# Second stage of a fused attention and two-layer expert kernel: loads of h moved to the queue of weights and stores, weights in four transfers, next pool opened with the last products' issue

## The chip, the cores and the metric

The kernel runs on one core of a Trainium2 chip. The metric is device time in microseconds (us) of one execution; lower is better. TensorE (PE) multiplies, its weight loads are PEld; ScalarE is ACT, VectorE is DVE, GpSimd is POOL, and SyncE (SP) issues transfers. ACTq and SPq are the transfers that ScalarE and SyncE issue.

## The reference

```python
x = attention(q, k, v)                       # 4 x 8 heads, 576 tokens of 64: pooled plus local part
x = x.transpose(0, 2, 1, 3).reshape(2304, 512)
h = (x @ w_a) * (x @ w_b)                    # 2304 x 1536
x2 = h @ w_out                               # 2304 x 512: the second stage here
h2 = x2 @ moe2_w_in                          # 2304 x 2048
out = (h2 * clip(h2 + 3, 0, 6) / 6) @ moe2_w_out
```

All in 32-bit floats. The inputs of the weights come as 64-bit words, which the kernel decodes.

## The kernel before

Each matrix product is made of three matmuls of split operands (`PASSES`): a tile holds a rounded first part (a copy by ScalarE) and the rest (a subtraction by VectorE). So each operand passes ScalarE, then VectorE, then TensorE.

The first stage makes attention and h, and stores h in DRAM, as 12 arrays `h_d[f]` of 128 rows and 2304 columns. The second stage (`second`, line 636) takes the tokens in five spans, four of 512 and one of 256. For each span it goes through f = 0 to 11: load 128 rows of h (`load`, line 641), the first part on ScalarE (line 647), the rest on VectorE (line 651), then 12 matmuls on TensorE into four banks of sums (`products`, line 659). A load of h is 256 KB, in the last span 128 KB. h has four buffers: three (`hg0`) that f = 0, 1, 2, 4, 5, 6, 8, 9, 10 take in turn, and one (`hg1`) for f = 3, 7, 11. Since that one is free later, the products run in the order 0, 1, 2, 4, 3, 5, 6, 8, 7, and so on. At a span's end ScalarE copies the four sums to `x2f` (line 676) and SyncE stores them (line 683).

Beside this the weights of the third and fourth stage are decoded: `decode` (line 223) loads 1 MB into a tile `raw` (two buffers, line 229), ScalarE makes `m` (line 237), and VectorE does six operations (lines 243 to 261). `pieces` (w2i) makes sums of quarters and splits them into `w2`; `staged` (w2o, line 1034) makes seven combinations in `ws` and stores them in DRAM (`w_d`, line 1065).

The third stage (`inner`, line 711) loads x2 in pairs of blocks (`x2r`, line 719), splits it into `in` (lines 699 and 702), and multiplies (`ph`, line 772); the fourth (`outer`) makes the output. Their tiles lie in the pool `p4`, which takes the place of the earlier pools of h, wo and raw. Before, it is opened behind the end of the last product, the issue of all stores of x2 and of all stores of w_d.

What sets the order: `Plan` holds every step with an engine, a planned duration, a due time (`want`), what it waits for, and buffers that it takes and gives. It runs the steps in planned time, on each engine the ready one with the smallest due time, and the instructions are issued in that order. Each engine, and each queue of transfers, keeps it. All transfers are planned on one queue, at 256 KB per us and 2.5 us more until they land, whichever engine issues them:

```python
def DMA(kb, want, run, after=(), take=(), give=()):
    i = plan.add("SP", dma(kb), want, run, after, take)
    j = plan.add("-", 0, want, lambda: None, [i], give=give, late=DMA_L)
    issued[j] = i
```

Before, the loads of h are planned so but issued by ScalarE, the others by SyncE. In the compiled program all transfers share eight completion counters, taken in turn: a transfer is not issued before the eighth ahead of it has landed.

Of the kernel before, what the change touches and what calls it, by code (L numbers as in the profile page):

```python
# [138 lines left out]
def fused_kernel(ctx: ExitStack, tc: tile.TileContext, qk, vt, vd, wab, wo, w2i, w2o, mask, out):  # L139
# [44 lines left out]
    def slot(pool, shape, dtype, tag, name):  # L184
        return pool.tile(shape, dtype, tag=tag, bufs=BUFS[tag], name=name)
# [8 lines left out]
    def act(n):  # L194
        return 0.1 + 0.00095 * n
# [26 lines left out]

    def decode(src, want, put, tag, after=(), ahead=4, slack=1.0, raw=None, queue=None):

        T = {}

        def load():
            T["raw"] = slot(xp if raw == "x" else dp, [P, W], mybir.dt.uint64, raw or "raw", "raw")
            (queue or nc.sync).dma_start(T["raw"].rearrange("p (a c) -> p a c", a=CUT), src.rearrange("a p c -> p a c"))

        def words():
            w = T["raw"].bitcast(U32).rearrange("p (n t) -> p n t", t=2)
            return w[:, :, 0], w[:, :, 1]
# [35 lines left out]


        i = DMA(1024, want - ahead, load, take=[raw or "raw"])
        i = ACT(act(W), want, magnitude, [i], take=["dm"], slack=slack)
        i = DVE(2 * dve2(W), want, exponent, [i])
# [9 lines left out]

    def pieces(src, want, where, raw=None):


        i, words = decode(src, want, None, None, slack=1.0, raw=raw)
        Q = W // CUT

# [347 lines left out]
    def second(n, f, want):  # L637
# [3 lines left out]
        def load():  # L641
            h = hs[n, f] = hg_slot(f, "h")[:, :, :nb]
            nc.scalar.dma_start(h[:, 1].bitcast(F32), h_d[f][:, lo:hi])

# [8 lines left out]
        def products():  # L653
            if f == 0:
                accs[n] = [bank("acc")[:, :nb] for _ in range(KC)]
            for e in range(KC):
# [4 lines left out]

        stored = [S_["h", m, f] for m in range(NBLK) if begin[m] < hi and begin[m] + sizes[m] > lo]
        i = DMA(nb // 2, want - 12, load, stored + [S_["p3" if f % 4 == 3 else "p2"]], take=[f"hg{f % 4 // 3}"])
        i = ACT(act(nb), want - 12, h_first, [i])
        i = DVE(dve(nb), want - 12, h_second, [i])
        i = S_["second", n, f] = PE(12 * (0.009 + 0.00044 * nb), want, products, [i, S_["wo", f // 2], S_["ps"]],
               take=["q"] * KC if f == 0 else [],
               give=[f"hg{f % 4 // 3}"] + (["wo"] if n == len(spans) - 1 and f % 2 else []))
        if f < F1 - 1:
            return  # L670
        for e in range(KC):
            T = {}

            def out_of(e=e, T=T):
                T["t"] = slot(pools["p3"], [P, NC], F32, "xo", "x2f")[:, :nb]
                nc.scalar.activation(T["t"], accs[n][e], AF.Copy)

            def store(e=e, T=T):
                for m in range(lo // NB, (hi - 1) // NB + 1):
                    if m not in x2_d:  # L680
                        x2_d[m] = dram.tile([KC, P, NB], F32, name=f"x2_d{m}")
                    a, b = max(lo, m * NB), min(hi, m * NB + NB)
                    nc.sync.dma_start(x2_d[m][e][:, a - m * NB:b - m * NB], T["t"][:, a - lo:b - lo])

            j = ACT(act(nb), want, out_of, [i], take=["xo"], give=["q"])
            j = DMA(nb // 2, want, store, [j], give=["xo"])
            for m in range(lo // NB, (hi - 1) // NB + 1):
                S_.setdefault(("x2d", m), []).append(j)
        S_["last second"] = i

# [19 lines left out]
    def inner(p, want, opened):  # L710
# [3 lines left out]

        def load(t, h):
            def run():
# [3 lines left out]
            return DMA(NB, want - 12 if p else want - 6, run,  # L720
                       S_["x2d", m[t]] + [S_["second", len(spans) - 1, 1] if p == 0 else opened],
                       take=["x0" if p == 0 else "L"])


        ld = {(h, t): load(t, h) for t, h in ((0, 0), (1, 0), (1, 1), (0, 1))}
        tag = "x0" if p == 0 else "L"
# [241 lines left out]
    for f in range(F1):  # L968
        S_["wab", f] = decode(wab[f], when[0, f] - 4, lambda f=f: wab_t.setdefault(f, slot(wpool, [P, 2, W], F32R, "wh", "wh")),
                              "wh", ahead=26 if f < 2 else 6, slack=0.0,  # L970
                                queue=None)
    for t, (n, f) in enumerate(jobs):
# [53 lines left out]
    for i in range(F2 // 2):  # L1026
        if i == 5:
            S_["p3"] = plan.add("-", 0, 0, open_p3, [S_["h", n, f] for n, f in jobs[-2:]] + [S_["raw x", k] for k in SPARE])
        S_["raw x", i] = pieces(w2i[i], T1 + 8 + 5.5 * i, place_of(i), "x" if i in SPARE else None)
        S_["w2i", i] = S_["raw x", i]  # L1030
# [4 lines left out]
    def staged(k, want):  # L1035
        i, words = decode(w2o[k], want, None, None, slack=1.0)
        T = {}
# [45 lines left out]
    for k, (n, f) in enumerate(steps):  # L1083
        second(n, f, T2 + k)
    T3 = T2 + len(steps)
    S_["p4"] = plan.add("-", 0, 0, open_p4, [S_["last second"]] +
                        [issued[x] for m in range(2 * PAIRS) for x in S_["x2d", m]] +
                        [issued[x] for k in range(F2 // 2) for x in S_["w_d", k]])
    for p in range(PAIRS):
# [91 lines left out]
```

## Time and profile before

| | us |
|---|---|
| three runs: median (lowest, highest) | 962.59 (960.75, 963.54) |
| the profiled execution | 964.17 |
| its span, first to last instruction | 962.2 |
| TensorE busy in the span | 932.5 (97%) |
| TensorE weight loads | 875.6 (91%) |
| VectorE | 755.3 (78%) |
| ScalarE | 455.8 (47%) |

The span is the time from the first to the last instruction that the profiler recorded; the 2.0 us between it and the execution's time lie around it. Busy times overlap: the engines work at the same time. TensorE's busy time holds the modelled ends of pipelined matmuls, so a stretch in which it is busy may still hold fewer matmuls than another of the same length.

### The profile page before, as it was taken

The numbers are of one execution on the slowest core, as the hardware profiler recorded it, in microseconds if no ns is written. First come the engines' busy times: TensorE is split into PE (matmuls) and PEld (weight loads), VectorE is DVE, ScalarE is ACT, GpSimd is POOL, SyncE is SP. The second block draws the span as 40 slices with busy tenths as digits, with TensorE's granted clock in tenths as the row PEclk, the third lists the DMA queues.
The fourth block names the chain that finished last, engine by engine and source line by source line (L and its number), as shares of the span: only waits on it lengthen the run. The fifth ranks groups of instructions, "written<-read, shape, count | busy, mean of one in ns | idle before, by whom it ended". The sixth has DMA issues, their size and how long they took to land.

```text
span 962.2 us, 18896 instructions
## 1 busy us (share of the span) xinstructions
PE 932.5 (97%) x7246; PEld 875.6 (91%) x7246; DVE 755.3 (78%) x1375; ACT 455.8 (47%) x1164; POOL 5.6 (1%) x44
## 2 busy tenths in 40 slices
PE   7899999999999999999999897999999999999998
PEld 6688989999899999997778687999999999999998
DVE  4999999824637969676787842999898999897983
ACT  4677445433645333323444432555454565554551
POOL 1000000000000000000000000000000000000000
PEclk9799999999999999999999999999999999999999
DMA  9645664424115524326768756334237891805401
GB/s 268 183 124 161 196 203 138 135 84 158 43 53 167 178 95 133 131 97 224 234 196 270 233 166 202 126 132 156 107 132 263 280 289 34 277 21 188 142 17 50
DMA packets 103146, 151.23 MB, mean 157 GB/s; under 512 B 8208, under 2 KB 71696, under 8 KB 103056
## 3 DMA queue, kind: packets, MB, share of 16 engines
q1 hardware_dynamic: 93728, 134.64, 43.4%
q10 hardware_dynamic: 9328, 15.39, 5.3%
q8 instruction: 57, 0.93, 0.4%
q14 instruction: 33, 0.27, 0.1%
HBM read 100.19 MB, written 49.81 MB: 156 GB/s over the span
## 4 chain that ended last, share of the span: by engine, by line
PE 84%; DVE 8%; DMA 6%; issue 1%; ACT 1%; ACTq 0%; SPq 0%; DVEq 0%
PE pab L602 32%; PE ph L772 18%; PE oacc L895 15%; PE acc L659 10%; DMA h<-h_d 4%; PE po L543 2%; PE dsc L398 2%; DVE in L702 2%; PE sc L496 1%; PE pt L529 1%; PE dpo L448 1%; DMA raw<-w2o 1%; DVE e L868 1%; PE po L539 1%; PE dpt L430 1%
## 5 line engine op out<-in xcount | busy, mean ns | idle before, releaser
L602 PE MATMUL pab<-x,wh 128*128 128x344 f32 (+2 forms) x2016 | 319.8, 317 | 0.1
L602 PEld LDWEIGHTS pab<-x,wh 128*128 128x128 f32 x2016 | 306.4, 188 | 3.6 <-issue 1.8
L895 PE MATMUL oacc<-w2o,in 128*128 128x256 f32 x1512 | 182.0, 283 | 1.4 <-DVE in L702 1.4
L895 PEld LDWEIGHTS oacc<-w2o,in 128*128 128x128 f32 x1512 | 181.3, 191 | 2.1 <-DVE in L702 2.0
L772 PE MATMUL ph<-in,w 128*128 128x384 f32 x1008 | 175.7, 335 | 2.2 <-ACT in L699 2.1
L772 PEld LDWEIGHTS ph<-in,w 128*128 128x128 f32 x1008 | 175.2, 188 | 2.7 <-ACT in L699 2.3
L659 PE MATMUL acc<-h,wo 128*128 128x512 f32 (+1 forms) x720 | 156.5, 378 | 10.7 <-ACT h L647 9.6
L659 PEld LDWEIGHTS acc<-h,wo 128*128 128x128 f32 x720 | 127.6, 193 | 39.7 <-ACT h L647 11.8
L788 DVE TENSOR_TENSOR part<-ph,part 128x384 f32<-128x384 f32 x168 | 86.0, 553 | 8.9 <-PE ph L772 8.2
L611 DVE TENSOR_TENSOR a<-a,pab 128x344 f32<-128x344 f32 (+2 forms) x84 | 41.4, 494 | 58.2 <-PE pab L602 43.3
L796 ACT ACTIVATE r<-part,three 128x384 f32<-128x384 f32 x96 | 56.3, 613 | 53.5 <-DVE part L788 51.1
L651 DVE TENSOR_TENSOR h<-h 128x512 fp32r<-128x512 f32 (+1 forms) x60 | 37.5, 636 | 49.1 <-ACT h L647 48.9
L608 ACT ACTIVATE a<-pab 128x344 f32<-128x344 f32 (+2 forms) x84 | 36.7, 443 | 79.4 <-PE pab L602 56.9
L699 ACT ACTIVATE in<-gr 128x384 fp32r<-128x384 f32 x96 | 47.5, 521 | 41.1 <-PE oacc L895 28.6
L647 ACT ACTIVATE h<-h 128x512 fp32r<-128x512 f32 (+1 forms) x60 | 34.8, 588 | 65.5 <-DMA h<-h_d 50.8
L237 ACT ACTIVATE m<-raw 128x1024 f32<-128x1024 f32 x34 | 39.2, 1153 | 51.1 <-DVE raw L255 26.0
L702 DVE TENSOR_TENSOR in<-gr,in 128x384 fp32r<-128x384 f32 x96 | 50.0, 560 | 7.0 <-ACT in L699 6.3
L699 ACT ACTIVATE in<-e 128x384 fp32r<-128x384 f32 x72 | 36.4, 526 | 34.0 <-PE oacc L895 19.5
L799 DVE SCALAR_TENSOR_TENSOR r<-r,part 128x384 f32<-128x384 f32 x96 | 50.6, 553 | 1.3 <-ACT r L796 1.1
L513 ACT ACTIVATE e<-sc,mx 128x64 f32<-128x64 f32 x160 | 48.0, 320 | 5.3 <-DVE mx L505 5.3
L255 DVE SCALAR_TENSOR_TENSOR raw<-raw,m 128x1024 f32<-128x1024 uint32 x34 | 41.7, 1227 | 1.2
L248 DVE SCALAR_TENSOR_TENSOR raw<-raw,m 128x1024 uint32<-128x1024 uint32 x34 | 41.5, 1221 | 0.2
(86 smaller groups left out, 900.5 us busy)
## 6 DMA issues: line engine op xcount, KB each, us to landing
g_d<-r SPq DMA_DIRECT2D x96, 192.0 KB, 2.1
gr<-g_d SPq DMA_DIRECT2D x48, 384.0 KB, 5.1
raw<-wab SPq DMA_DIRECT2D x12, 1024.0 KB, 11.9
h<-h_d ACTq DMA_DIRECT2D x48, 256.0 KB, 3.8
h_d<-a SPq DMA_DIRECT2D x48, 172.0 KB, 2.0
raw<-w2i SPq DMA_DIRECT2D x8, 1024.0 KB, 5.5
raw<-w2o SPq DMA_DIRECT2D x8, 1024.0 KB, 7.3
qk<-qk SPq DMA_DIRECT2D x14, 576.0 KB, 5.9
```

The lines of the kernel that those rows point to most:

```text
L248: nc.vector.scalar_tensor_tensor(out=hi, in0=hi, scalar=0xC0000000, in1=T["m"].bitcast(U32), op0=ALU.bitwise_and, op1=ALU.bitwise_or)
L255: nc.vector.scalar_tensor_tensor(out=lo.bitcast(F32), in0=lo, scalar=2.0 ** -52, in1=m, op0=ALU.mult, op1=ALU.mult)
L513: nc.scalar.activation(L["e"][:, p, h], L["s4"][:, p, h], AF.Exp, bias=L["mx"][:, p, h:h + 1], scale=SCALE, accum_out=L["z"][:, p, h:h + 1])
L602: nc.tensor.matmul(T[k], wab_t[f][:, x, c], xs[n][:, g, y, :nb], start=(g == 0 and i == 0), stop=(g == KC - 1 and i == 2))
L659: nc.tensor.matmul(accs[n][e], wo_t[f // 2][:, x, c], hs[n, f][:, y], start=(f == 0 and i == 0), stop=(f == F1 - 1 and i == 2))
L699: nc.scalar.activation(x[0][:, 0], src(), AF.Copy)
L702: nc.vector.tensor_tensor(x[0][:, 1], src(), x[0][:, 0], op=ALU.subtract)
L772: nc.tensor.matmul(acc[k], t[:, x, g * P:(g + 1) * P], X[k, g][0][:, y], start=(g == 0 and n == 0), stop=(g == 1 and n == 2))
L788: nc.vector.tensor_tensor(s[name], acc[k], s[other], op=ALU.add)
L796: nc.scalar.activation(T["r"], src(), AF.Relu, bias=three)
L799: nc.vector.scalar_tensor_tensor(out=T["r"], in0=T["r"], scalar=6.0, in1=src(), op0=ALU.min, op1=ALU.mult)
L895: nc.tensor.matmul(acc[n][e], X[n, k][0][:, x, e * P:(e + 1) * P], t[:, y], start=(k == 0 and i == 0), stop=(k == K - 1 and i == 2))
```

## The change

The loads of h are issued by SyncE, and their due time is 40 steps ahead of the product's instead of 12; ScalarE's and VectorE's part of h are due 14 steps ahead instead of 12. All eight weights w2o and the last four of the eight w2i are loaded in four transfers of 256 KB, which take their places in the queue one by one; `m` waits for all four. The last three products of the last span are planned as issued early, and `p4` is opened behind the issue of the last one, no longer behind its end; the last span's four `x2f` lie in `p4`. The four loads of x2r for the first pair are tied to four products (the eighth, tenth and so on from the last wide span on) instead of one.

```diff
@@ decode @@
-    def decode(src, want, put, tag, after=(), ahead=4, slack=1.0, raw=None, queue=None):
+    def decode(src, want, put, tag, after=(), ahead=4, slack=1.0, raw=None, step=CUT):
...
-        def load():
-            T["raw"] = slot(xp if raw == "x" else dp, [P, W], mybir.dt.uint64, raw or "raw", "raw")
-            (queue or nc.sync).dma_start(T["raw"].rearrange("p (a c) -> p a c", a=CUT), src.rearrange("a p c -> p a c"))
+        def load(a, b):
+            def run():
+                if a == 0:
+                    T["raw"] = slot(xp if raw == "x" else dp, [P, CUT, W // CUT], mybir.dt.uint64, raw or "raw", "raw")
+                nc.sync.dma_start(T["raw"][:, a:b], src[a:b].rearrange("a p c -> p a c"))
+            return run
...
-        i = DMA(1024, want - ahead, load, take=[raw or "raw"])
-        i = ACT(act(W), want, magnitude, [i], take=["dm"], slack=slack)
+        i, loads = None, []
+        for a in range(0, CUT, step):
+            i = DMA(256 * step, want - ahead, load(a, a + step), [i and issued[i]], take=[] if a else [raw or "raw"])
+            loads.append(i)
+        i = loads
+        i = ACT(act(W), want, magnitude, i, take=["dm"], slack=slack)
@@ second @@
-            nc.scalar.dma_start(h[:, 1].bitcast(F32), h_d[f][:, lo:hi])
+            nc.sync.dma_start(h[:, 1].bitcast(F32), h_d[f][:, lo:hi])
...
-        i = DMA(nb // 2, want - 12, load, stored + [S_["p3" if f % 4 == 3 else "p2"]], take=[f"hg{f % 4 // 3}"])
-        i = ACT(act(nb), want - 12, h_first, [i])
-        i = DVE(dve(nb), want - 12, h_second, [i])
-        i = S_["second", n, f] = PE(12 * (0.009 + 0.00044 * nb), want, products, [i, S_["wo", f // 2], S_["ps"]],
-               take=["q"] * KC if f == 0 else [],
-               give=[f"hg{f % 4 // 3}"] + (["wo"] if n == len(spans) - 1 and f % 2 else []))
+        i = DMA(nb // 2, want - 40, load, stored + [S_["p3" if f % 4 == 3 else "p2"]], take=[f"hg{f % 4 // 3}"])
+        i = ACT(act(nb), want - 14, h_first, [i])
+        i = DVE(dve(nb), want - 14, h_second, [i])
+        busy = 12 * (0.009 + 0.00044 * nb)
+        end = n == len(spans) - 1
+        take, give = ["q"] * KC if f == 0 else [], [f"hg{f % 4 // 3}"]
+        if end and f >= F1 - 3:
+            i = S_["issued", f] = PE(0.01, want - 3, products, [i, S_["wo", f // 2], S_["ps"], S_.get(("issued", f - 1))],
+                                     take=take, slack=-PE_L)
+            i = PE(busy, want, lambda: None, [i], give=give)
+        else:
+            i = PE(busy, want, products, [i, S_["wo", f // 2], S_["ps"]], take=take, give=give)
+        S_["second", n, f] = i
         if f < F1 - 1:
             return
+        if end:
+            S_["p4"] = plan.add("-", 0, 0, open_p4, [S_["issued", f]] +
+                                [issued[x] for m in range(2 * PAIRS) for x in S_.get(("x2d", m), [])] +
+                                [issued[x] for k in range(F2 // 2) for x in S_["w_d", k]])
...
-                T["t"] = slot(pools["p3"], [P, NC], F32, "xo", "x2f")[:, :nb]
+                T["t"] = (slot(pools["p4"], [P, NB], F32, "c", "x2f") if end else
+                          slot(pools["p3"], [P, NC], F32, "xo", "x2f"))[:, :nb]
...
-            j = ACT(act(nb), want, out_of, [i], take=["xo"], give=["q"])
-            j = DMA(nb // 2, want, store, [j], give=["xo"])
+            tag = "c" if end else "xo"
+            j = ACT(act(nb), want, out_of, [i, S_["p4"] if end else None], take=[tag], give=["q"])
+            j = DMA(nb // 2, want, store, [j], give=[tag])
@@ inner @@
-                       S_["x2d", m[t]] + [S_["second", len(spans) - 1, 1] if p == 0 else opened],
+                       S_["x2d", m[t]] + [S_["second", *divmod((len(spans) - 2) * F1 + 8 + 2 * n, F1)] if p == 0 else opened],
@@ the main body @@
-        S_["raw x", i] = pieces(w2i[i], T1 + 8 + 5.5 * i, place_of(i), "x" if i in SPARE else None)
+        S_["raw x", i] = pieces(w2i[i], T1 + 8 + 5.5 * i, place_of(i), "x" if i in SPARE else None,
+                               1 if i > 3 else CUT)
...
-        i, words = decode(w2o[k], want, None, None, slack=1.0)
+        i, words = decode(w2o[k], want, None, None, slack=1.0, step=1)
...
-    S_["p4"] = plan.add("-", 0, 0, open_p4, [S_["last second"]] +
-                        [issued[x] for m in range(2 * PAIRS) for x in S_["x2d", m]] +
-                        [issued[x] for k in range(F2 // 2) for x in S_["w_d", k]])
```

What the change moves: on SyncE, where the second stage begins (h_d_93 to h_d_104 are f = 0 to 11; raw is a weight, w_d the store of ws). Before:

```order
L614 DMA h_d_104<-a 128x344 x2
L1065 DMA w_d_111<-ws 128x4x256
L1065 DMA w_d_111<-ws 128x3x256
L229 DMA raw<-w2o 128x4x256
L229 DMA raw<-w2i 128x4x256
L1065 DMA w_d_111<-ws 128x4x256
L1065 DMA w_d_111<-ws 128x3x256
L229 DMA raw<-w2o 128x4x256
```

and in the changed kernel:

```order
L621 DMA h_d_104<-a 128x344 x2
L650 DMA h<-h_d_97 128x512
L650 DMA h<-h_d_96 128x512
L1085 DMA w_d_111<-ws 128x4x256
L650 DMA h<-h_d_98 128x512
L1085 DMA w_d_111<-ws 128x3x256
L650 DMA h<-h_d_99 128x512
L231 DMA raw<-w2o 128x256
L650 DMA h<-h_d_101 128x512
L231 DMA raw<-w2o 128x256 x2
L650 DMA h<-h_d_100 128x512
L231 DMA raw<-w2o 128x256
```

Loads of h now stand between the stores, and the weight (one row of 128x4x256 before) is in quarters between them. ScalarE at the same place had them before between its own work:

```order
L608 ACTIVATE a<-pab 128x344
L643 DMA h<-h_d_97 128x512
L1048 ACTIVATE ws<-raw 128x256
L1051 ACTIVATE ws<-raw 128x512
L643 DMA h<-h_d_96 128x512
L647 ACTIVATE h<-h 128x512
L643 DMA h<-h_d_98 128x512
L647 ACTIVATE h<-h 128x512
L309 ACTIVATE w_5048<-raw 128x256
```

In the changed kernel no such row stands on ScalarE. In the last span (loads of h of 128x256) SyncE had before:

```order
L1065 DMA w_d_112<-ws 128x3x256
L683 DMA x_d_6245<-x2f 128x384
L683 DMA x_d_6247<-x2f 128x128
L683 DMA x_d_6245<-x2f 128x384
L683 DMA x_d_6247<-x2f 128x128
L719 DMA x2r<-x_d_5527 128x2x384
L719 DMA x2r<-x_d_5529 128x2x384 x2
L719 DMA x2r<-x_d_5527 128x2x384
L683 DMA x_d_6247<-x2f 128x256 x4
```

and has in the changed kernel, from the load of f = 0 on:

```order
L650 DMA h<-h_d_93 128x256
L231 DMA raw<-w2o 128x256
L739 DMA x2r<-x_d_5518 128x2x384
L650 DMA h<-h_d_104 128x512
L231 DMA raw<-w2o 128x256
L650 DMA h<-h_d_94 128x256
L231 DMA raw<-w2o 128x256 x2
L650 DMA h<-h_d_95 128x256
L739 DMA x2r<-x_d_5520 128x2x384
L650 DMA h<-h_d_97 128x256
L739 DMA x2r<-x_d_5520 128x2x384
L650 DMA h<-h_d_96 128x256
```

The x2r loads and the last weight's quarters (raw) now stand among the last span's loads of h. On ScalarE, at the stage's end, before:

```order
L643 DMA h<-h_d_104 128x256
L647 ACTIVATE h<-h 128x256 x3
L676 ACTIVATE x2f<-acc 128x256 x4
L699 ACTIVATE in<-x2r 128x384 x4
L780 ACTIVATE part<-ph 128x384 x3
L699 ACTIVATE in<-x2r 128x384 x4
L780 ACTIVATE part<-ph 128x384
```

and now:

```order
L719 ACTIVATE in<-x2r 128x384 x2
L696 ACTIVATE x2f<-acc 128x256 x4
L719 ACTIVATE in<-x2r 128x384 x2
L800 ACTIVATE part<-ph 128x384 x3
L719 ACTIVATE in<-x2r 128x384 x4
```

Two `in` of the third stage, each the first part of half a pair's block, moved ahead of the four copies of the last span's sums. On TensorE all instructions keep their order but for one product: the twelve matmuls of f = 0 of the last span stand ahead of those of f = 11 of the span before.

## Rows read from the trace of the kernel before

**Rows 1.** The page, the chain that ended last by line, shares of the span.

```profile
PE pab L602 32%; PE ph L772 18%; PE oacc L895 15%; PE acc L659 10%; DMA h<-h_d 4%; PE po L543 2%; PE dsc L398 2%; DVE in L702 2%; PE sc L496 1%; PE pt L529 1%; PE dpo L448 1%; DMA raw<-w2o 1%; DVE e L868 1%; PE po L539 1%; PE dpt L430 1%
```

**Rows 2.** Busy time by stretch (us:us): length, engines, granted clock, DMA share, GB/s.

```profile
430.00:600.00 170.00, 157.19 (x724) 127.79 (x722) 110.84 (x174) 65.97 (x116) 0.00 (x0) 0.98 0.68 216
600.00:775.00 175.00, 174.89 (x1006) 174.89 (x1007) 162.46 (x323) 91.76 (x171) 0.00 (x0) 1.00 0.52 173
```

**Rows 3.** Groups by line and shape, TensorE, 430 to 600: busy us, mean ns | idle.

```profile
L659 PE MATMUL acc<-h,wo 128*128 128x512 f32 x576 | 136.8, 397 | 7.0 <-ACT h L647 6.1 <-DVE h L651 0.9
L659 PE MATMUL acc<-h,wo 128*128 128x256 f32 x144 | 19.9, 300 | 3.7 <-ACT h L647 3.5
```

**Rows 4.** Busy time by stretch, TensorE alone, inside the second stage.

```profile
536.00:571.00 35.00, 35.00 (x154) 1.00 0.64 203
574.00:580.50 6.50, 6.50 (x57) 1.00 0.75 232
479.20:482.50 3.30, 3.30 (x9) 0.50 0.29 102
592.00:595.00 3.00, 3.00 (x16) 0.50 0.00 0
```

**Rows 5.** Timeline of TensorE: start us, us, instruction [idle before <-releaser].

```profile
430.21 19.81 PE L659 MATMUL acc<-h,wo 128*128 128x512 f32 x84
451.01 0.50 PE L659 MATMUL acc<-h,wo 128*128 128x512 f32 x1 [0.99 <-ACT h L647]
451.73 25.01 PE L659 MATMUL acc<-h,wo 128*128 128x512 f32 x107 [0.23 <-DVE h L651]
478.08 0.50 PE L659 MATMUL acc<-h,wo 128*128 128x512 f32 x1 [1.34 <-ACT h L647]
...
591.06 6.40 PE L659 MATMUL acc<-h,wo 128*128 128x256 f32 x36 [2.54 <-ACT h L647]
599.52 0.44 PE L772 MATMUL ph<-in,w 128*128 128x384 f32 x1 [2.06 <-ACT in L699]
```

**Rows 6.** Waits, 425 to 605: us in total, times, longest.

```profile
ACT h L647 <- DMA h<-h_d: 49.5, 25, 5.9
```

**Rows 7.** Timeline of all engines, before the first and the last stop.

```profile
437.27 0.67 SPq L229 DMA_DIRECT2D raw<-w2o  x1
...
438.84 0.33 ACTq L643 DMA_DIRECT2D h<-h_d  x1
...
444.93 0.63 ACT L647 ACTIVATE h<-h 128x512 fp32r<-128x512 f32 x1 [3.87 <-DMA h<-h_d]
444.99 0.81 ACTq L643 DMA_DIRECT2D h<-h_d  x2
...
450.32 1.24 ACT L647 ACTIVATE h<-h 128x512 fp32r<-128x512 f32 x2 [3.35 <-DMA h<-h_d]
...
582.13 2.38 SPq L719 DMA_DIRECT2D x2r<-x_d  x4
...
584.40 3.05 ACTq L643 DMA_DIRECT2D h<-h_d  x3
...
590.59 1.11 ACT L647 ACTIVATE h<-h 128x256 fp32r<-128x256 f32 x3 [5.86 <-DMA h<-h_d]
```

**Rows 8.** Transfers: issues of 430 to 600, then line 643: durations ns, landings.

```profile
h<-h_d ACTq DMA_DIRECT2D x45, 256.0 KB, 4.0
raw<-w2o SPq DMA_DIRECT2D x7, 1024.0 KB, 7.3
...
L643 ACTq DMA_DIRECT2D h<-h_d x57: 326/327/952, 433.5 to 587.1; - x57
...
DMA to landing us min/median/max: 2.4/4.0/7.3
```

**Rows 9.** Busy time by stretch, and the queues of 722 to 770 (q1 is SyncE's).

```profile
735.00:740.00 5.00, 5.00 (x31) 5.00 (x30) 3.11 (x6) 1.49 (x2) 0.00 (x0) 1.00 1.02 342
...
q1 hardware_dynamic: 10346, 13.01, 82.6%
```

**Rows 10.** Waits of SyncE's queue, 430 to 600.

```profile
SPq L1065 <- DVE ws L1054: 58.6, 10, 18.7
```

More of the change, by code (lines that the diff above doesn't have):

```diff
@@ L221, in fused_kernel @@
     pools = {}
-    def decode(src, want, put, tag, after=(), ahead=4, slack=1.0, raw=None, queue=None):
+    def decode(src, want, put, tag, after=(), ahead=4, slack=1.0, raw=None, step=CUT):
         T = {}
-        def load():
-            T["raw"] = slot(xp if raw == "x" else dp, [P, W], mybir.dt.uint64, raw or "raw", "raw")
-            (queue or nc.sync).dma_start(T["raw"].rearrange("p (a c) -> p a c", a=CUT), src.rearrange("a p c -> p a c"))
+        def load(a, b):
[4 more added lines that the diff above has]
+            return run
         def words():
-            w = T["raw"].bitcast(U32).rearrange("p (n t) -> p n t", t=2)
+            w = T["raw"].rearrange("p a c -> p (a c)").bitcast(U32).rearrange("p (n t) -> p n t", t=2)
             return w[:, :, 0], w[:, :, 1]
@@ L282, in fused_kernel, with pieces @@
     takers = {}
-    def pieces(src, want, where, raw=None):
-        i, words = decode(src, want, None, None, slack=1.0, raw=raw)
+    def pieces(src, want, where, raw=None, step=CUT):
+        i, words = decode(src, want, None, None, slack=1.0, raw=raw, step=step)
         Q = W // CUT
@@ L683, in store @@
                     nc.sync.dma_start(x2_d[m][e][:, a - m * NB:b - m * NB], T["t"][:, a - lo:b - lo])
-            j = ACT(act(nb), want, out_of, [i], take=["xo"], give=["q"])
-            j = DMA(nb // 2, want, store, [j], give=["xo"])
+            tag = "c" if end else "xo"
+            j = ACT(act(nb), want, out_of, [i, S_["p4"] if end else None], take=[tag], give=["q"])
+            j = DMA(nb // 2, want, store, [j], give=[tag])
             for m in range(lo // NB, (hi - 1) // NB + 1):
                 S_.setdefault(("x2d", m), []).append(j)
-        S_["last second"] = i
     PAIRS = NT // (2 * NB)
@@ L713, in inner, with load @@
         raw, X, ready = {}, {}, {}
-        def load(t, h):
+        def load(n, t, h):
             def run():
@@ L720, in load @@
             return DMA(NB, want - 12 if p else want - 6, run,
-                       S_["x2d", m[t]] + [S_["second", len(spans) - 1, 1] if p == 0 else opened],
+                       S_["x2d", m[t]] + [S_["second", *divmod((len(spans) - 2) * F1 + 8 + 2 * n, F1)] if p == 0 else opened],
                        take=["x0" if p == 0 else "L"])
-        ld = {(h, t): load(t, h) for t, h in ((0, 0), (1, 0), (1, 1), (0, 1))}
+        ld = {(h, t): load(n, t, h) for n, (t, h) in enumerate(((0, 0), (1, 0), (1, 1), (0, 1)))}
         tag = "x0" if p == 0 else "L"
@@ L969, in fused_kernel @@
         S_["wab", f] = decode(wab[f], when[0, f] - 4, lambda f=f: wab_t.setdefault(f, slot(wpool, [P, 2, W], F32R, "wh", "wh")),
-                              "wh", ahead=26 if f < 2 else 6, slack=0.0,
-                                queue=None)
+                              "wh", ahead=26 if f < 2 else 6, slack=0.0)
     for t, (n, f) in enumerate(jobs):
```

## The prediction

> **What bounds the kernel now.** I read the chain of waits first. TensorE's lines are most of it, and one entry is not an engine's: the loads of h from DRAM, 4% of the span [rows 1]. They belong to the second stage, so I cut the span at 430 and 600 us: TensorE is busy 157.19 of 170 us there, but 174.89 of 175 in the stage behind it [rows 2]. Hence two readings: only the second stage has anything to give, and what it saves comes through whole, because the third stage is full of matmuls and only starts earlier.
>
> How much can the stage give? It issues 576 matmuls of 512 columns and 144 of 256 [rows 3]. Where nothing disturbs them they pass at 35.00 us for 154, 0.227 us each, and 6.50 us for 57, at most 0.12 us each [rows 4]. The floor is 576 x 0.227 + 144 x 0.12 = 130.8 + 17.3 = 148.1 us. The stage begins at 430.21; the last matmul of its last run ends at 591.06 + 6.40 = 597.46 by the modelled end, about 597.3 by its pace [rows 5]. That is 167.1 us: **19.0 us above the floor**. Then TensorE is idle 2.06 us more, waiting for ScalarE's `in`, before the third stage's first matmul [rows 5]. Pool: 21.1 us.
>
> What ends the idle time? In all six long stops it is ScalarE's h (the first and last stand in [rows 5]; 9.6 us together, the 6.1 and 3.5 in [rows 3]). Each stop costs more than its idle time: the second matmul after 451.01 starts 0.72 us later instead of 0.227, since it needs VectorE's half of h. And twice the granted clock stood at 0.50 right after a stop: 9 matmuls in 3.30 us, and 16 narrow ones in 3.00 us [rows 4], 1.3 and 1.1 us more than at full pace in these windows. ScalarE itself stood 49.5 us for the landing of h, in 25 waits [rows 6]: it is late because the load is.
>
> Why is the load late? The first stop shows it: SyncE issues 1 MB of w2o at 437.27, ScalarE a load of h at 438.84, and that lands only at about 444.9, when ScalarE's h runs; the next load, standing behind that instruction on ScalarE, is issued after it, at 444.99, and read at 450.32 [rows 7]. The last stop is alike: four x2r loads at 582.13, three h loads at 584.40, read at 590.59 [rows 7]. The median landing of h is 4.0 us, from 2.4 to 7.3; 1 MB of weights takes 7.3 [rows 8]. So h loses twice: its issue waits behind ScalarE's own work, and its bytes mix with a megabyte that is not urgent.
>
> **The change part by part.**
>
> *h's loads leave ScalarE for SyncE's queue, planned 28 steps earlier.* There are still three buffers for h and one for every fourth. A buffer comes free when its product ends and is needed three products later, 3 x 12 x 0.227 = 8.2 us. Landing 4.0, ScalarE 0.63 (the h instruction of 444.93 in [rows 7]), VectorE about 0.7 (451.01 to 451.73 in [rows 5]) and some 0.3 of hand-offs make 5.6: **2.6 us of slack**, if nothing holds the issue. Each load costs its issuer 0.33 us [rows 8]; 57 of them are 19 us taken from ScalarE, which is not the bound (65.97 of 170 busy [rows 2]). I cost that gain at nothing itself.
>
> *Weights in four transfers.* Eight w2o and four w2i become 48 transfers instead of 12. The bytes stay; a load of h now has 256 KB ahead of it where it had 1 MB. At 342 GB/s, which SyncE's queue reached alone [rows 9], 256 KB are 0.8 us. SyncE issues 57 + 36 = 93 more; four issues of x2r took 2.38 us [rows 7], so at 0.33 to 0.6 each 31 to 56 us of a queue with 148 us. The bytes: 216 GB/s over 170 us [rows 2] are 36.7 MB, at 342 GB/s 107 us of 148. Against cutting speaks a rule of the Trainium skill, "DMA: Bandwidth & Descriptors", section "Rules for kernel authors": few transfers of 1 MiB or more for bandwidth, many small ones are to be merged. What it would make of the sum is the last rival. The trace speaks against it here: the quickest load of h lands in 2.4 us [rows 8], and the program lets eight transfers be under way at once.
>
> *Spans of 512 columns.* From 430.21 they run to 573.9 (the narrow matmuls fill the window from 574 [rows 4]): 143.7 us against a floor of 130.8, 12.9 lost. Bounds of what remains: 0 and 12.9. Nearer to 0, since the order of the changed queue puts every h load where its buffer comes free, with one or two quarters or stores ahead of it, so 2.6 us of slack stand against 0.8 to 1.6 us of queue. I take **4.0 left**, for one or two places where ScalarE's `m` waits for a last quarter in front of an h: gain 8.9.
>
> *The last span.* 23.4 us (573.9 to 597.3) against 17.3: 6.1 lost. Here a product takes 12 x 0.12 = 1.44 us, so the slack is 3 x 1.44 = 4.3 minus some 3.5 (landing at its quickest, 2.4 [rows 8]; ScalarE and VectorE about 0.4 each, as the three of 590.59 [rows 7]; hand-offs): 0.8 at best, and below zero with the median landing of 4.0. The change also brings the last weight, three x2r loads and the stores into this piece: from the first narrow load to the last, 33 transfers of 6.9 MB, 20 us at 342 GB/s, for some 28 us of products around it. Bounds 0 and 6.1, and I take the middle, **3.0 left**: gain 3.1.
>
> *The next pool is opened with the last products' issue.* ScalarE's first two `in` now stand before the four copies of the last sums, and their x2r has long landed; the stop of 2.06 us [rows 5] goes but for a hand-off: gain **2.1**, bounds 1.5 and 2.1. What is late next is `in` for the second product: its work stands behind the copies, as before.
>
> *The other edits* (the last span's results in the new pool's buffers, x2r spread over the queue) are in these terms. The first stage keeps its order on TensorE: nothing.
>
> Sum: 8.9 + 3.1 + 2.1 = 14.1 us. The profiled execution took 964.17: 950.1. It lies 1.6 above the median of the runs, so **948.5** is my number.
>
> **The rivals.**
>
> *Half.* The stops move rather than go: the last span keeps its 6.1, the wide spans half of 12.9, and only the transition is won: 6.4 + 2.1 = 8.5, 954.1 (951 to 958). For it: the last span has no slack. Against: four of the six stops lie in the wide spans, where there is slack.
>
> *No change in effect.* The number of buffers, not the place in the queue, sets when a load can start; if loads were issued as early as buffers allow already, only the queue differs: 962.6 (959.8 to 965.4). Against: the load read at 450.32 was held by ScalarE, not by a buffer.
>
> *Slower: the head of the one queue.* A queue issues in order. SyncE stood 58.6 us in 10 waits of w_d stores for VectorE, 5.9 each, the longest 18.7 [rows 10]; nothing urgent was behind them. Now h is. If these waits stay at 5.9, each exceeds the slack of 2.6 by 3.3: 33 us of new stops for 19.0 lost, less 2.1: +12, 974 (966 to 985). It decides when the mean wait passes 2.6 + 2.1 = 4.7. Against: the queue now reaches such a store later, since the h loads before it wait for their buffers, and VectorE's instruction for it stands behind an h two or three products older than the one queued behind the store.
>
> *Slower: the quarters cost.* If each of the 36 extra transfers took its 2.4 us alone, 86 us come to the 116 that the engines were busy (0.68 of 170 [rows 2]): 202 us for the stage, +35, 998. The rule of the Trainium skill named above is the one by which this would come. Against: loads that overlap in the trace, as the three of 584.40 that are all read at 590.59 [rows 7].
>
> **How the numbers follow.** Forecast 0.66 (943 to 953), half 0.17, no effect 0.08, head of the queue 0.07, quarters 0.02. A measurement of this kernel can tell about 0.3%, 2.9 us. The first two are faster: 0.83; same 0.08; slower 0.09. The range of 8 in 10 takes all of the forecast and most of the half: 942 (everything of the pool gone, from the median 941.5) to 959.
>
> **What would show it.** Right: between the second stage's start and the third's first matmul about 155 us instead of 169; ScalarE's waits for the landing of h far below 49.5 us; the landing's maximum near 5; no clock of 0.50 in the stage; the idle time before `ph` under 0.6 us; the third stage's 175 us unchanged. Wrong: TensorE still stopping for h with the load issued late behind a w_d or x2 store (head of the queue), or issued in time and landing late (bytes), or the stage shorter and the third longer.

## The result, and the profile after

The changed kernel took **947.83 us** (median of four runs, 946.96 to 948.64); the kernel before, on the same chip, 961.90 (960.75 to 963.54). The ratio is 0.9831, 95% interval 0.9803 to 0.9858; the plain quotient of the two medians is 0.9854, inside the interval. The profiled execution took 948.64 us, its span is 946.8.

Where did the time go? First TensorE's timeline of the second stage (start us, us, first instruction of the stretch, count, [idle before <-releaser]), to be read against [rows 5]:

```profile
431.87 131.49 PE L666 MATMUL acc<-h,wo 128*128 128x512 f32 x577
563.69 16.18 PE L666 MATMUL acc<-h,wo 128*128 128x512 f32 x119 [0.33 <-DVE h L658]
580.68 3.70 PE L666 MATMUL acc<-h,wo 128*128 128x256 f32 x24 [0.81 <-ACT h L654]
584.22 15.96 PE L792 MATMUL ph<-in,w 128*128 128x384 f32 x91
```

577 matmuls run through in one stretch where there were four long stops, and `ph` follows the last product with no idle time. From the stage's first matmul to the first `ph` it was 599.52 - 430.21 = 169.3 us; now it is 584.22 - 431.87 = **152.35**. The groups by line and shape in the same stage say the same, beside [rows 3]:

```profile
L666 PE MATMUL acc<-h,wo 128*128 128x512 f32 x576 | 133.0, 392 | 0.3 <-DVE h L658 0.3
L666 PE MATMUL acc<-h,wo 128*128 128x256 f32 x144 | 18.7, 286 | 1.0 <-ACT h L654 0.8
```

ScalarE ended 6.1 and 3.5 us of idle time before; now 0 and 0.8. The stretches of [rows 2] (busy us of TensorE, its weight loads, VectorE, ScalarE and GpSimd, granted clock, DMA share, GB/s):

```profile
430.00:600.00 170.00, 168.72 (x824) 143.19 (x824) 126.80 (x202) 75.40 (x135) 0.00 (x0) 1.00 0.72 223
600.00:775.00 175.00, 175.00 (x1049) 175.00 (x1048) 163.90 (x329) 94.65 (x176) 0.00 (x0) 1.00 0.58 196
```

TensorE now fills the first stretch as it fills the second. What is saved comes through whole: from the first `ph` to the span's end it was 962.2 - 599.5 = 362.7 us, now 946.8 - 584.2 = 362.6. The stage won 17.0 us, and not the whole of it is in the span, because this execution entered the stage 1.7 us later (431.87, not 430.21; the last section shows why). In the chain that ended last, the loads of h fall from 4% to 1% of the span [rows 1]:

```profile
PE pab L609 32%; PE ph L792 16%; PE oacc L915 15%; PE acc L666 14%; PE po L550 2%; PE dsc L405 2%; DVE in L722 2%; PE sc L503 1%; PE pt L536 1%; PE dpo L455 1%; DVE w2o L1120 1%; DMA h<-h_d 1%; DVE e L888 1%; DVE part L808 1%; PE po L546 1%
```

The waits (us in total, times, longest), of ScalarE first and then of SyncE's queue, answer to [rows 6] and [rows 10]:

```profile
ACT h L654 <- DMA h<-h_d: 63.5, 39, 3.8
```

```profile
SPq L650 <- PE acc L666: 71.9, 48, 2.5
...
SPq L1085 <- DVE ws L1074: 1.5, 1, 1.5
```

ScalarE waits *more* for h than before, 63.5 us against 49.5, though TensorE hardly stops for it; only the longest wait fell, from 5.9 to 3.8. SyncE's queue stands before a load of h until TensorE gives a buffer back, in 48 of 57 loads, and its long waits for the store of `ws` are gone. The transfers themselves, beside [rows 8] (durations of the issue in ns; landing in us, min/median/max):

```profile
L650 SPq DMA_DIRECT2D h<-h_d x57: 319/320/456, 435.1 to 578.1; - x57
...
DMA to landing us min/median/max: 2.1/3.0/4.3
```

### The profile page after: what moved, and what is told of

Same layout as the page of the kernel before. It is cut to its first block, busy times and chain, and to the rows that moved or that the text cites. A ratio compares the mean times of both kernels' runs of the same rounds, so it can differ in the third digit from the quotient of the medians.

```text
span 946.8 us, 19011 instructions
## 1 busy us (share of the span) xinstructions
PE 927.8 (98%) x7246; PEld 874.9 (92%) x7246; DVE 756.0 (80%) x1375; ACT 456.3 (48%) x1164; POOL 5.4 (1%) x44
## 4 chain that ended last, share of the span: by engine, by line
PE 86%; DVE 10%; DMA 1%; issue 1%; ACT 1%; SPq 0%; DVEq 0%; ACTq 0%
PE pab L609 32%; PE ph L792 16%; PE oacc L915 15%; PE acc L666 14%; PE po L550 2%; PE dsc L405 2%; DVE in L722 2%; PE sc L503 1%; PE pt L536 1%; PE dpo L455 1%; DVE w2o L1120 1%; DMA h<-h_d 1%; DVE e L888 1%; DVE part L808 1%; PE po L546 1%
## 5 line engine op out<-in xcount | busy, mean ns | idle before, releaser
L666 PE MATMUL acc<-h,wo 128*128 128x512 f32 (+1 forms) x720 | 151.2, 371 | 1.3 <-ACT h L654 0.8
L666 PEld LDWEIGHTS acc<-h,wo 128*128 128x128 f32 x720 | 125.7, 188 | 26.8 <-DVE h L658 1.7
L654 ACT ACTIVATE h<-h 128x512 fp32r<-128x512 f32 (+1 forms) x60 | 35.1, 589 | 81.5 <-DMA h<-h_d 63.5
## 6 DMA issues: line engine op xcount, KB each, us to landing
w2o<-w_d SPq DMA_DIRECT2D x14, 512.0 KB, 10.1
```

The lines of the kernel that those rows point to most:

```text
L666: nc.tensor.matmul(accs[n][e], wo_t[f // 2][:, x, c], hs[n, f][:, y], start=(f == 0 and i == 0), stop=(f == F1 - 1 and i == 2))
```

## The experiments

One number helps to read them. For each of the 44 products from the fifth to the 48th I took, from the profile's instructions, the time from the end of the product four before (it frees the buffer) to the end of VectorE's half of h. Call it h's **lag**; with four buffers it must stay under three wide products, 8.2 us. The table has its parts too, as means: from the release to the load's issue, and from the issue to the start of ScalarE's half. "Stage" is the time from the stage's first matmul to the first `ph`, in one profiled execution each; ratios are to the kernel before, run on the same chip (its medians were 961.9 to 964.0, so ratios are compared, not times). Plain quotients of medians differ from these ratios by up to 0.2% (the change 0.9854, weights whole 0.9826, due times 12 0.9835, pool late 0.9849), so these four versions are not told apart by their times.

| kernel | ratio (95%) | stage | release to issue | issue to ScalarE | lag: mean, largest, over 8.2 |
|---|---|---|---|---|---|
| before | 1 | 169.3 | 0.88 | 4.56 | 7.4, 11.9, 14 of 44 |
| due times only | 0.9951 (0.9930–0.9971) | 160.5 | 0.62 | 4.41 | 7.2, 10.4, 11 |
| quarters only | 0.9908 (0.9890–0.9926) | 161.1 | 0.43 | 4.12 | 6.5, 10.1, 7 |
| queue only | 0.9920 (0.9900–0.9940) | 160.6 | 0.23 | 4.06 | 6.3, 10.0, 5 |
| queue and due times | 0.9862 (0.9833–0.9890) | 156.6 | 0.14 | 4.09 | 6.4, 9.5, 5 |
| change, h on ScalarE | 0.9891 (0.9872–0.9910) | 158.1 | 0.28 | 4.03 | 5.9, 10.2, 2 |
| change, weights whole | 0.9825 (0.9805–0.9845) | 153.9 | 0.14 | 4.00 | 6.2, 9.7, 4 |
| change, due times 12 | 0.9837 (0.9814–0.9860) | 153.9 | 0.14 | 3.60 | 5.7, 9.5, 3 |
| change, pool late | 0.9848 (0.9829–0.9867) | 154.0 | 0.05 | 3.44 | 5.1, 6.7, 0 |
| the change | 0.9831 (0.9803–0.9858) | 152.4 | 0.07 | 3.50 | 5.2, 6.9, 0 |
| change, 64 KB pieces | 0.9988 (0.9973–1.0004) | 161.6 | 2.05 | 3.46 | 7.4, 9.3, 14 |

In the change, and in the versions of it with h on ScalarE, pool late and 64 KB pieces, the 48th product is the narrow one that the order puts ahead, so the last wide product lies outside the 44: its lag is 7.4 us in the change and 11.1 with h on ScalarE. That order is part of what an edit can move: the issuing engine changes nothing in the plan, but due times and quarters do (with weights whole or due times 12 the narrow product stands behind f = 11 again, as before).

### Taking one part out of the change

*The loads of h go back to ScalarE, in their new places:*

```diff
-            nc.sync.dma_start(h[:, 1].bitcast(F32), h_d[f][:, lo:hi])
+            nc.scalar.dma_start(h[:, 1].bitcast(F32), h_d[f][:, lo:hi])
```

> The changed kernel with the loads of h issued by ScalarE again, due 40 steps ahead as in the change, weights still in quarters. Theory (a load of h is late for two reasons: its issue stands behind ScalarE's own work, and a megabyte mixes with it): the second reason is gone, the first is back, so about half of the 14 us returns: 953 to 957, with stops of TensorE in the wide spans again, ended by h. Rival, the bytes alone: 947 to 949. Rival, the place of the issue alone: 959 to 962.

Measured: 953.54 us, 0.9891, in the expected range. In TensorE's timeline stops of the old kind are back, all in the last 30 us of the stage (the 552 matmuls before them run through):

```profile
559.20 0.49 PE L666 MATMUL acc<-h,wo 128*128 128x512 f32 x1 [1.28 <-ACT h L654]
...
566.30 11.61 PE L666 MATMUL acc<-h,wo 128*128 128x512 f32 x83 [1.91 <-DVE h L658]
...
587.04 2.02 PE L666 MATMUL acc<-h,wo 128*128 128x256 f32 x12 [2.25 <-ACT h L654]
```

The landing's median is no worse than in the change (2.8 us, there 3.0; the longest 5.3, there 4.3). The load's issue is worse, up to 3.5 us after the buffer came free. Not all of that is ScalarE's own work. The loads issued at 552.36 and 554.68, 2.7 and 2.3 us late, stood for the completion counter that all transfers share: the transfer eight ahead landed at 552.27 and 554.58. The one of 558.69, 3.5 us late, stood behind `m`, which waited until 558.33 for a quarter of a weight. SyncE's queue waits for `ws` again:

```profile
SPq L1085 <- DVE ws L1074: 55.7, 11, 16.8
```

So these waits are idle time of a queue with nothing to do; where the loads of h stand in it, it waits for their buffers instead.

*The weights stay whole, in 1 MB transfers:*

```diff
-                               1 if i > 3 else CUT)
+                               CUT)
-        i, words = decode(w2o[k], want, None, None, slack=1.0, step=1)
+        i, words = decode(w2o[k], want, None, None, slack=1.0, step=CUT)
```

> The changed kernel with every weight in one transfer of 1 MB again, in the same one queue. Theory: a megabyte ahead of an h takes 3.1 us at 342 GB/s, 0.5 more than the slack of 2.6, so short stops at some of the eleven weights of the stage: 950 to 954, and the longest landing of h near 7 instead of 4.3. Rival, the place of the issue alone: 947 to 949. Rival, the bytes alone: 959 to 962.

Measured: 947.28 us, 0.9825: no difference from the change that can be measured, and the expectation missed. The landing's maximum is as long as it ever was:

```profile
DMA to landing us min/median/max: 2.4/3.1/7.9
```

and four products still have a lag over 8.2, but the stage is longer by 1.6 us only, in one profile each. A load that lands late by itself costs little when it was issued the moment its buffer came free.

*Due times back to 12:*

```diff
-        i = DMA(nb // 2, want - 40, load, stored + [S_["p3" if f % 4 == 3 else "p2"]], take=[f"hg{f % 4 // 3}"])
-        i = ACT(act(nb), want - 14, h_first, [i])
-        i = DVE(dve(nb), want - 14, h_second, [i])
+        i = DMA(nb // 2, want - 12, load, stored + [S_["p3" if f % 4 == 3 else "p2"]], take=[f"hg{f % 4 // 3}"])
+        i = ACT(act(nb), want - 12, h_first, [i])
+        i = DVE(dve(nb), want - 12, h_second, [i])
```

> The changed kernel with the due times of before (load, ScalarE's and VectorE's part of h all 12 steps ahead). Theory: in the changed kernel SyncE stood 71.9 us, 48 times, at a load of h for the end of a product, so the buffer sets the issue and the earlier due time only keeps other transfers from standing before it: 948 to 951. Rival, the due time carries the gain: 957 to 962.

Measured: 948.13 us, 0.9837. In the expected range; again 1.5 us in the stage of one profile, and nothing in the medians.

*The pool opened at its old place, the last results in the old pool:*

```diff
-        end = n == len(spans) - 1
+        end = False
...
```

> The changed kernel with the next pool opened where it was before (behind the end of the last product and the issue of all stores) and the last span's results in the old pool. Theory: the stop of 2.1 us before the third stage returns and nothing else: 949.5 to 950.5, TensorE idle some 2 us before its first ph. Rival, the pool is hidden by the rest: 947.5 to 948.2. Rival, the pool also carries part of the last span's gain: above 951.

Measured: 949.46 us, 0.9848, at the lower edge of the expected range; by the times it cannot be told from the change. The timeline shows the price, the stop of [rows 5] at its old length, and in one profile each the stage is 1.7 us longer:

```profile
584.11 0.44 PE L792 MATMUL ph<-in,w 128*128 128x384 f32 x1 [2.06 <-ACT in L719]
```

### One part alone, put into the kernel before

*The queue* (the first diff's line the other way round, in the kernel before, and nothing else):

> The kernel before with one edit: the loads of h are issued by SyncE; weights whole, due times and pool as before. Theory, as the first four runs leave it (with SyncE issuing, neither quarters nor the due time matter, the pool is worth 2): all but the pool's part, 948.5 to 951, the six long stops gone but for one or two. Rival, each edit alone is too little and they only work together: 954 to 960. Rival, the head of the queue (h behind w_d stores, weights whole, due late): above 960.

Measured: 954.55 us, 0.9920; a miss: it is half of the change and not nearly all, and lies where the rival "each edit alone is too little" put it. TensorE still stops for h in three places, and its largest lag is 10.0:

```profile
527.42 45.81 PE L659 MATMUL acc<-h,wo 128*128 128x512 f32 x227 [1.56 <-DVE h L651]
574.32 6.32 PE L659 MATMUL acc<-h,wo 128*128 128x256 f32 x48 [1.10 <-ACT h L647]
582.45 6.31 PE L659 MATMUL acc<-h,wo 128*128 128x256 f32 x36 [1.80 <-ACT h L647]
```

The first of these stops is of the head of the queue's kind: the load for it was issued at 519.59, 2.2 us after its buffer came free, behind a store of `ws`.

*The quarters* (the new `decode` with step 1 for the same weights, h on ScalarE):

> The kernel before with one edit: all w2o and the last four w2i in quarters; h issued by ScalarE with its old due time. Theory (the place of the issue is the cause, a megabyte only makes it worse): a part of the gain, 955 to 960, with stops still ended by h. Rival, the bytes are the cause: 948 to 952. Rival, more transfers cost: 963 to 968.

Measured: 953.62 us, 0.9908, better than expected but short of what the bytes alone were to give. *The due times* (40 and 14 in the kernel before):

> The kernel before with one edit: the due times of h (40 and 14 instead of 12); ScalarE issues, weights whole. Theory: an earlier due time on ScalarE puts the load's issue, which waits for a buffer, in front of more of ScalarE's work: 956 to 964, anything between little gain and none. Rival, the due time carries what the run with ScalarE issuing had gained: 953 to 955.

Measured: 957.24 us, 0.9951 (six runs), in the expected range. *The queue and the due times:*

> The kernel before, with the loads of h issued by SyncE and the due times of 40 and 14, weights whole and the pool opened at its old place. Alone the two gave 954.55 and 957.24. Theory, h is late only where the time from a buffer's release to its use exceeds three products (8.2 us), and any two parts bring that time under it: 949 to 951, as with the quarters added (949.46). Rival, the quarters are needed beside the queue: 952 to 955.

Measured: 950.82 us, 0.9862, in the expected range, but not for the reason given: five products still have a lag over 8.2 us, the longest 9.5, so the two parts thin the tail and do not end it. Its stage still holds the pool's 2 us at the end.

What follows from the eight together: the parts do not add. By the stages of one profile each, each alone takes 8 to 9 us of the 17.0; by the ratios the queue takes 7.7 and the quarters 8.9, but the due times only 4.7 (their profiled execution was the fastest of the six). All three with the old pool take 15.3. Due times added to the queue bring 4.0 more. But with h on ScalarE, due times and quarters together, less the pool's 2.1 us, leave about 160.2, hardly better than the quarters alone at 161.1. The lag says why. A product stops only where it passes 8.2 us: at a mean of 7.4 that is 14 of 44; the queue or the quarters alone bring the mean to 6.3 or 6.5 and the count to 5 or 7, the due times to 7.2 and 11. What remains is the tail: the largest lag is 9.3 us or more in every row of the table but two, the change and the late pool.

### Smaller pieces

*Sixteen transfers of 64 KB for each of those weights, each a step of the plan* (rows of 512 bytes):

```diff
-        for a in range(0, CUT, step):
-            i = DMA(256 * step, want - ahead, load(a, a + step), [i and issued[i]], take=[] if a else [raw or "raw"])
+            for a in range(4 * CUT):
+                i = DMA(64, want - ahead, part(a), [i and issued[i]], take=[] if a else [raw or "raw"])
...
```

> The changed kernel with those weights in sixteen transfers of 64 KB (512 bytes in each row) instead of four: 192 transfers for 12 weights. Theory, from 48 transfers that cost nothing against 12: SyncE's issue at 0.32 to 0.45 us each makes 144 more x 0.4 = 58 us, which still has room in the stage's 152 beside some 50 now, but an h may find eight small ones ahead of it: 948 to 953. Rival, transfers of this size lose bandwidth, and the DMA engines become the bound: above 958, with a DMA share near 1 in the stage.

Measured: 991.86 us, 1.0308 (1.0284 to 1.0331), a miss. The time is on the rival's side, but not for its reason. The stage takes 191.3 us, with stops like these:

```profile
598.93 13.18 PE L679 MATMUL acc<-h,wo 128*128 128x256 f32 x95 [6.12 <-DVE h L671]
...
628.58 11.71 PE L805 MATMUL ph<-in,w 128*128 128x384 f32 x53 [11.34 <-ACT in L732]
```

The engines of the transfers were busy 0.63 of 428 to 583, less than in the change (0.76), so it is not their bandwidth. But 144 more steps shift the order of every engine. So I made the same pieces inside the four old steps:

```diff
-                nc.sync.dma_start(T["raw"][:, a:b], src[a:b].rearrange("a p c -> p a c"))
+                if step < CUT:
+                    n = W // CUT // 4
+                    for c in range(0, W // CUT, n):
+                        nc.sync.dma_start(T["raw"][:, a, c:c + n], src[a][:, c:c + n])
...
```

> The changed kernel, where each of a weight's four steps issues four transfers of 64 KB (rows of 512 B) one behind another; the plan's steps, and with them the order on every engine, stay as in the changed kernel. The run with sixteen steps per weight took 991.86 us, but it changed the plan's order everywhere as well. Theory, the small transfers themselves are dear (144 more issues of 0.43 us on SyncE's queue, in front of loads of h and of stores): 965 to 995. Rival, the cost was that of the changed order: 947 to 952.

Measured: 962.63 us, 0.9988 (0.9973 to 1.0004): between the two. By the ratios the sixteen steps cost 46 us and the same pieces in the old order 15: a third is the pieces, the rest came with the changed order. The pieces' own third can be named. Once issued, h is as quick as in the change (3.46 and 3.50 us in the table); but it is issued 2.05 us after its buffer came free, not 0.07. Line 234 is the weights' issue:

```profile
L234 SPq DMA_DIRECT2D raw<-w2o x128: 328/430/921, 385.2 to 575.9; - x128
L234 SPq DMA_DIRECT2D raw<-w2i x64: 333/430/1807, 369.2 to 498.1; - x64
```

192 issues of 0.43 us are 83 us of SyncE, where the change has 48 of 0.42, 20 us (32 of w2o and the last 16 of w2i). The chain that ended last now has SyncE's issue in it, 5% of the span:

```profile
PE pab L614 28%; PE ph L797 16%; PE oacc L920 15%; SPq L234 5%; DMA h<-h_d 3%; PE acc L671 2%; PE po L555 2%; PE dpo L460 2%; PE dsc L410 2%; DVE in L727 2%; PE sc L508 1%; PE pt L541 1%; DMA raw<-w2o 1%; DVE e L893 1%; DVE w2o L1125 1%
```

The stage is 9.3 us longer than in the change, and begins 4.9 later, mostly because the first stage, too, stopped once (4.2 us at 400.88, for ScalarE's `a`, and then 3.4 us at a granted clock of 0.50). Together that is 14.2 us; by the ratios it is 15.

### The buffers, and the last span

*Three buffers for h:*

```diff
-        return slot(pools["p3" if f % 4 == 3 else "p2"], [P, 2, NC], F32R, f"hg{f % 4 // 3}", name)
+        return slot(pools["p2"], [P, 2, NC], F32R, "hg0", name)
...
```

> The changed kernel with three buffers for h in place of four. Theory, the slack is the products of the other buffers: it falls from 8.2 to 5.45 us (wide) and from 4.3 to 2.9 (narrow). In the profile of the changed kernel 15 of 44 wide products had a time from release to readiness above 5.45, by 9.0 us in sum, and a narrow product with a lag of 4.6 would come each (4.6+1.44)/3 = 2.0 us instead of 1.5, 6 us for twelve: 955 to 966, about 961. Rival, the buffers are not what the loads wait for: 947 to 950.

Measured: 954.60 us, 0.9895 (0.9869 to 0.9922), 0.4 below the expected range and far from the rival. The stage takes 160.8 us, 8.5 more; the stops are spread over it:

```profile
456.03 11.20 PE L666 MATMUL acc<-h,wo 128*128 128x512 f32 x48 [0.65 <-DVE h L658]
...
509.24 68.53 PE L666 MATMUL acc<-h,wo 128*128 128x512 f32 x323 [1.45 <-DVE h L658]
...
583.12 7.86 PE L666 MATMUL acc<-h,wo 128*128 128x256 f32 x48 [1.62 <-ACT h L654]
```

The lag counted from the release, now three products before, has a mean of 5.2 us, close to the slack of two products, 5.45, and 13 of 44 products are above that. So in the change the buffers set when a load starts, and the fourth is needed.

*Five spans of about equal width:*

```diff
-    cuts = list(range(0, NT, NC)) + [NT]
+    cuts = list(range(0, NT, 464)) + [NT]
...
```

(the last span's wider results take larger buffers of the same pool)

> The changed kernel with spans of 464, 464, 464, 464 and 448 tokens in place of four of 512 and one of 256. Theory, the last stops of the stage stand in the narrow span, whose slack of 4.3 us is less than the mean lag: with equal spans the slack is 3 x 2.48 = 7.4 us in all of them, above the largest lag of 6.9, and 1 to 2 us go: 945.5 to 947.5. Rival, the wider last results (two stores each) come later to the third stage, or the wide products at the end delay its first ones: 948 to 951.

Measured: 951.19 us, 0.9865 (0.9841 to 0.9890), just above the rival's range; its interval still touches the change's. The timeline shows both halves:

```profile
524.31 30.42 PE L666 MATMUL acc<-h,wo 128*128 128x464 f32 x144 [1.94 <-DVE h L658]
556.17 29.37 PE L666 MATMUL acc<-h,wo 128*128 128x448 f32 x143 [1.43 <-DVE h L658]
586.58 0.44 PE L792 MATMUL ph<-in,w 128*128 128x384 f32 x1 [1.04 <-ACT in L719]
```

Inside the last span there is no stop any more, as the slack said. But there are new ones where a span begins, and `ph` waits 1.0 us, since `in` now runs behind the four copies of wider sums. At the stop of 524.31 the trace shows what VectorE was doing:

```profile
517.22 0.59 ACT L654 ACTIVATE h<-h 128x464 fp32r<-128x464 f32 x1 [0.51 <-PE acc L666]
...
522.49 1.22 DVE L264 TENSOR_TENSOR raw<-raw 128x1024 f32<-128x1024 f32 x1
...
523.62 1.74 DVE L658 TENSOR_TENSOR h<-h 128x464 fp32r<-128x464 f32 x3
```

ScalarE's half of this h was done at 517.81; VectorE took it up 5.8 us later, after its work on a weight. The stop of 556.17 is alike (done at 550.30, taken up at 555.50). Why the plan put the weight's work ahead there stays open. No version here is clearly quicker than the change; weights whole, due times 12 and pool late cannot be told from it by their times.

## Why the prediction was right, and where its steps were off

*The pool* was right: 19.0 above the floor and 2.06 before `ph`, all of it in the second stage, and what it gave came through whole.

*Wide spans.* "4.0 left" was too much. To the end of the last wide product, 2.3 us are left over the floor (566.35 - 431.87 = 134.5 for 576 wide and 12 narrow matmuls, which the order puts ahead of it, 132.2 at [rows 4]'s pace). The reason given, that every load is issued where its buffer comes free, is what the runs show: 41 of the 44 loads were issued within 0.1 us of it. The places where `m` would hold up an h did not cost what I set aside.

*Last span.* "3.0 left" measured 2.0 (584.22 - 566.35 = 17.9 for 132 matmuls, 15.8 at pace). The slack below zero was right: its stop for h is the one long stop left, 0.81 us. It is also the head of the queue, in small:

```profile
575.79 0.49 SPq L703 DMA_DIRECT2D x_d<-x2f  x1
...
576.38 0.36 SPq L650 DMA_DIRECT2D h<-h_d  x1
...
580.21 0.42 ACT L654 ACTIVATE h<-h 128x256 fp32r<-128x256 f32 x1 [2.43 <-DMA h<-h_d]
```

The load of 576.38 was issued 1.2 us after its buffer came free, behind stores of x2, and read 3.8 us later.

*Pool opened early.* 2.1 was right: the stop is gone, and comes back at 2.06 when this part alone is undone. The times cannot show it.

*The sum.* 14.1 us were predicted of the stage and the transition; they gave 17.0, since the wide spans gave 1.7 and the last span 1.0 more than the sum had. The later start of this execution took back 1.7 in the profile. That is how 950.1 for the profiled execution and the 948.64 it took lie so near, and it is luck: two terms were too small, and a fall of the clock that has nothing to do with the change hid part of it. The medians, 961.90 and 947.83, also differ by 14.1, but the profiled execution of before, 964.17, took longer than all four runs behind that median, so this agreement is partly chance too.

*The quarters.* The step took them as needed, "256 KB ahead of it where it had 1 MB". That failed: beside the other parts they are worth 1.6 us in the profile and nothing in the medians. They are worth 0.9% in the kernel before, where h is on ScalarE and due late. The rule of the Trainium skill, "DMA: Bandwidth & Descriptors", section "Rules for kernel authors", asks for 1 MiB or more in a transfer and counts those under 64 KB as mostly overhead; the pieces of 64 KB stand at that edge. At 256 KB the traces show no cost of cutting; at 64 KB there is one, 1.6% with the order kept, but it is the issuing engine's 0.43 us for each, not the transfers, which landed in 2.4 us (median).

*Queue.* That h loses twice was right, and both losses have a size now: of the mean lag's fall from 7.4 to 5.2 us, 0.8 is the issue and 1.1 the way to ScalarE's half; the rest, 0.3, lies between there and the end of VectorE's half. The Trainium skill, "DMA: Bandwidth & Descriptors", section "Issuing engines are not separate DMA queues", says that starting transfers on several engines saves only issue time, usually small. As to bandwidth no run here speaks against it: the landing's median is 2.8 us with two issuers and 3.0 with one. But moving 57 loads to another issuer was worth 0.8% alone: not for their 0.33 us each, but for the work that stood ahead of them.

*Rivals.* Half: no, the wide spans gave 10.6 of their 12.9. No effect: its reason, that buffers set the start, is true of the kernel after (48 waits for TensorE, and three buffers cost 6 us by the ratios). Of the one before it is true in part: 27 of its 44 loads were issued within 0.1 us of the release, the others up to 5.2 us after it. Head of the queue: the waits for `ws` fell from 58.6 to 1.5 us; one stop of its kind is left, the one above. Quarters: quicker alone, not slower.

*What would show it.* The stage at about 155 (152.4), the landing's maximum near 5 (4.3), no clock of 0.50 in the stage, no idle time before `ph`, the third stage's 175 us unchanged: all so. One sign was wrong: "ScalarE's waits for the landing of h far below 49.5 us". They rose to 63.5. ScalarE comes to h earlier now and waits for each load in its turn; that it waits says nothing about TensorE. The lag, or TensorE's idle time with its releaser, is the sign to read.

## What to carry to other kernels

Where an engine is fed through a ring of buffers, measure for each use the time from the release of the buffer to the data's readiness, split at the load's issue, and compare its tail, not its mean, with the products that the other buffers cover. Several remedies for one tail do not add up: test them in pairs, and do not add up what each one gives alone (here 4.7 to 8.9 us of 16 by the ratios). Put a load where nothing that can be late stands ahead of it, and count the issues on that queue before cutting anything smaller.

## What the runs showed that was not expected

The granted clock. With the pool late, TensorE stopped 2.06 us before `ph`, and right after it ran at a granted clock of 0.51, which is the lower of its two levels, 1.2 GHz (ten matmuls in 3.3 us):

```profile
584.70:588.00 3.30, 3.29 (x10) 3.29 (x11) 2.64 (x5) 1.31 (x3) 0.00 (x0) 0.51 0.78 257
```

From the first `ph` to the end that execution needed 948.2 - 584.1 = 364.1 us, 1.5 more than the change. So such a stop can cost nearly twice its length. It does not always: behind stops of 2.25, 2.07 and 2.04 us at the end of the stage (h on ScalarE, due times only, queue and due times) the granted clock stayed at 1.00. In the profile of the change the same happened in the first stage, at a place that the change does not touch, behind a stretch in which TensorE was busy about half of the time:

```profile
120.00:123.40 3.40, 1.78 (x17) 1.40 (x17) 3.40 (x6) 0.60 (x3) 0.00 (x0) 1.00 0.84 230
123.40:126.80 3.40, 3.40 (x13) 3.40 (x13) 3.33 (x6) 0.32 (x1) 0.00 (x0) 0.50 1.03 374
```

In the profile of before, the same two stretches ran at 1.00, and so they did in five versions of the change (h on ScalarE, weights whole, due times 12, pool late, three buffers). This is the 1.7 us by which the second stage began later; it belongs to the execution, not to the change.
